# Attention and two feed-forward layers: three places each for keys, queries and values, loads asked for when free, scores first in a step, x's parts apart, later exponents in a buffer of their own

## The chip, the cores and the metric

The kernel runs on one core of a Trainium2 chip. The metric is the device time of one execution in microseconds (us). The core has five engines with instruction queues of their own, each worked off in program order: TensorE (PE, matrix products; its weight loads are shown as PEld), VectorE (DVE), ScalarE (ACT), GpSimd (POOL) and SyncE (SP), which here issues all DMA loads. An instruction that must wait for another engine holds everything behind it on its own engine. Matrix products land in PSUM, which has eight banks here called 0 to 7; everything else lies in SBUF.

## The reference

Windowed attention over 2 batches, 8 heads, 768 positions, head size 64, then two feed-forward layers. Cut to what matters:

```python
scores = scale * q @ k.T                  # per batch and head
keep = (key < n_global) | ((0 <= rel) & (rel < n_local))      # n_global 8, n_local 96
scores = where(keep, scores - slope[h] * dist, -1e9)
a = exp(scores - max(scores)); a = a / (sum(a) + 1e-9)
x = (a @ v) laid out as 1536 tokens x 512
h = x @ w_in;  x = (h * tanh(softplus(h))) @ w_out            # first layer, d_ff 2048
h = x @ w_in2; g = 0 if h <= -1, h if h >= 1, else (h + 1)**2 / 4
out = g @ w_out2                                              # second layer, d_ff 2048
```

The weights come as 64-bit floats, viewed as int64.

## The kernel before

**Attention.** Two heads make a pair; there are eight pairs (four per batch), and each takes three steps of two query blocks of 128, so the loop has 24 steps and runs from s = -1 to 27 (L383). The first block of a sequence sees 128 keys, all others 256 (`keys`, L302). A step passes through a pipeline whose stages work on different steps in one turn of the loop: in turn s, PE multiplies the transposed weights of step s-3 with the values (`values`, L376), transposes the weights of step s-2 (`transposes`, L358) and makes the scores of step s+1 (`scores`, L321), in this order. The scores have two pairs of PSUM banks, (0, 1) and (6, 7), used in turn. DVE adds the bias and takes the minimum (`softmax`, L333); ACT takes the exponential with its sum (L338); DVE makes the reciprocal of the sum of step s-1 (`normalise`, L343 and L344) and POOL multiplies with it (L348); ACT and DVE copy the transposed weights from PSUM, the first block by ACT, the second by DVE (`evict`, L363). A product of weights and values that is complete for 512 or 256 tokens is put on the list `done`; at the end of the same turn `split` (L407) rounds it to a high part on ACT (`rounded`, L169) and makes the low part, the remainder, on DVE (`remainder`, L174): x_hi and x_lo.

**Loads.** `load_qk` brings the keys and queries of a pair, `load_v` its values (L95, L96, L101). Pair (0, 0) has its keys and queries in a pool of its own; all else takes places in `a_raw`, two per kind (L283). Ahead of the loop stand the keys and queries of pair 1 and the values of pairs 0 and 1. In the loop, turn s = 3i asks for keys and queries of pair i+1 and turn 3i+2 for values of pair i+1; so the values of pair 1 are asked for a second time, in turn 2. SP issues the loads in program order, and a load waits until its place is free.

**Weights.** A weight tile holds 128 columns of w_in and 128 rows of w_out as 64-bit words; there are 16 for each layer. `Weights.load` (L201) brings one into one of two places (`stage`; a third place for tile 2), and `convert` makes float32 from the words in two halves i: `top` scales the upper 32 bits (L161, or on POOL L165), in place; `low` makes the bits that are shifted in from below (L223, ACT); `sign` takes the sign bit from the top 16 bits of the same word (L227, DVE); `value` combines the three in `wbits` (L230, DVE); `high` rounds (L169) and `rest` makes the remainder (L174). `wbits` has two places, taken in turn; the second also holds the distance tables of the attention bias at first. Three tiles (PRE) are converted inside the attention loop, at the turns that BESIDE (L36) lists: Tfi, Bfi, Vfi, Hfi and Rfi are top, low, sign with value, high and rest of half i of tile f; b2 to b7 are biases of heads, h and g the first pieces of the feed-forward part. On POOL are top and rest there (FIRST_ON); for tiles 3 to 15 top and high are on ACT and rest on DVE (LATER_ON).

**Feed-forward.** Each layer and batch takes 16 hidden tiles f; in period n PE makes h of tile n (L509, L510, L512, 768 tokens as 512 and 256) and the output products of tile n-1 (L560 in the first layer, L569 in the second). The gate of a tile of the first layer (`mish`) is a chain over ACT and DVE: exponential (L518), L520 and L521 on DVE, logarithm (L522) and exponential (L524) on ACT, the product with h on DVE (L525), and the product of the two (L528) on DVE; then ACT rounds g (L547) and DVE makes its remainder (L549). L525 is the last to read h, and frees its banks for the next tile. Tiles 3 to 15 of the first layer are converted beside the gates of the first 13 periods (`due`, L675), in three portions: after L525 come `begin` (the last tile's second rounding, top 0, low 0, sign 0), after L528 `middle` (the last tile's second remainder, value 0), after L549 `end` (top 1, low 1, sign 1, high 0, value 1, the next load, rest 0). Each engine runs these in the order in which the program writes them.

## Time and profile before

| what | us |
|---|---|
| three runs | 656.35, 651.24, 654.9 |
| their median | 654.9 |
| the profiled execution | 658.07 |
| its span, first to last instruction | 656.3 |
| busy in the span: PE, PEld, DVE, ACT, POOL | 622.4, 519.5, 414.7, 394.6, 57.7 |
| mean granted clock of TensorE, as a share of full speed | 0.988 |

The profile is of one execution. Busy time is the time in which an engine has an instruction in work; instructions overlap a little on one engine, so a group's sum can be more than the time that it takes. "Idle before" in a row is the time in which the engine had nothing to do just before that instruction, with the instruction that ended the wait behind an arrow. A wait for several things is put down to the one that came last.

### The profile page before, as it was taken

What the parts mean: (1) busy time and instruction counts of PE and PEld (TensorE: products, weight loads), DVE (VectorE), ACT (ScalarE), POOL (GpSimd) and SP (SyncE); (2) the same over time, 40 slices, a digit from 0 to 9 for tenths busy, and PEclk for the clock granted to TensorE, in tenths of its full rate; (3) what the DMA queues carried; (4) which work ended last, traced back from release to release, by engine and by line L of the source; (5) the groups of instructions that cost most, each with busy time, mean ns of one, the idle gap of its engine ahead of it and who ended that gap; (6) DMA issues with size and microseconds to landing.
All of it is one profiled execution on the core that took longest, in us unless ns stands there. A gap on an engine that the chain in (4) does not pass through costs nothing.

```text
span 656.3 us, 9854 instructions
## 1 busy us (share of the span) xinstructions
PE 622.4 (95%) x3600; PEld 519.5 (79%) x3600; DVE 414.7 (63%) x1019; ACT 394.6 (60%) x892; POOL 57.7 (9%) x122
## 2 busy tenths in 40 slices
PE   5687979999999999999999999999999999999996
PEld 4465657887877788888888888888888888888885
DVE  6487875888888897777777764766643433333332
ACT  5478874877787766666666665777733433333333
POOL 3546752000000000000000000000000000000000
PEclk9899989999999999999999999999999999999999
DMA  7955630133223310211111110233100100000002
GB/s 243 261 166 162 190 109 1 65 128 129 88 105 129 129 65 1 65 64 57 54 53 52 56 52 22 108 128 129 64 1 1 61 36 0 1 1 0 1 1 100
DMA packets 10567, 50.58 MB, mean 77 GB/s; under 512 B 1424, under 2 KB 1680, under 8 KB 6416
## 3 DMA queue, kind: packets, MB, share of 16 engines
q1 hardware_dynamic: 10512, 49.88, 23.1%
q8 instruction: 30, 0.49, 0.3%
q14 instruction: 25, 0.20, 0.1%
HBM read 46.73 MB, written 3.15 MB: 76 GB/s over the span
## 4 chain that ended last, share of the span: by engine, by line
PE 68%; DVE 16%; ACT 9%; DMA 3%; issue 2%; SPq 1%; POOL 0%; DVEq 0%; ACTq 0%; POOLq 0%
PE psum L569 20%; PE psum L560 12%; PE psum L509 11%; PE psum L510 11%; PE psum L512 10%; DVE wbits L230 3%; DVE e L521 3%; DVE wlo L174 2%; ACT pr L338 2%; DVE wbits L227 2%; DVE g_lo L549 2%; ACT qr L524 2%; PE psum L376 2%; PE psum L358 2%; DMA qr<-in_q_dram 2%
## 5 line engine op out<-in xcount | busy, mean ns | idle before, releaser
L534 DVE TENSOR_SCALAR e<-e 128x512 f32<-128x512 f32 x64 | 23.0, 360 | 121.3 <-ACT e L533 121.3
L533 ACT ACTIVATE e<-psum 128x512 f32<-128x512 f32 x64 | 30.8, 481 | 96.8 <-PE psum L512 96.8
L509 PE MATMUL psum<-x_hi,whi 128*128 128x512 f32 (+1 forms) x256 | 83.6, 343 | 3.7 <-DVE e L525 3.7
L509 PE MATMUL psum<-y_hi,whi 128*128 128x512 f32 (+1 forms) x256 | 82.4, 338 | 0.0
L510 PE MATMUL psum<-x_lo,whi 128*128 128x512 f32 (+1 forms) x256 | 82.3, 338 | 0.0
L510 PE MATMUL psum<-y_lo,whi 128*128 128x512 f32 (+1 forms) x256 | 82.0, 336 | 0.0
L569 PE MATMUL psum<-whi,g_hi 128*128 128x512 f32 x192 | 75.1, 391 | 0.0
L569 PE MATMUL psum<-wlo,g_hi 128*128 128x512 f32 x192 | 75.1, 391 | 0.0
L569 PE MATMUL psum<-whi,g_lo 128*128 128x512 f32 x192 | 74.7, 389 | 0.0
L549 DVE TENSOR_TENSOR g_lo<-e,g_hi 128x512 fp32r<-128x512 f32 (+1 forms) x128 | 65.5, 552 | 12.8 <-ACT g_hi L547 12.8
L547 ACT ACTIVATE g_hi<-e 128x512 fp32r<-128x512 f32 (+1 forms) x128 | 60.1, 517 | 22.3 <-DVE e L528 14.4
L560 PE MATMUL psum<-g_lo,whi 128*128 128x512 f32 (+1 forms) x256 | 69.2, 351 | 0.3
L560 PE MATMUL psum<-g_hi,whi 128*128 128x512 f32 (+1 forms) x256 | 65.8, 338 | 0.0
L560 PE MATMUL psum<-g_hi,wlo 128*128 128x512 f32 (+1 forms) x256 | 65.7, 338 | 0.0
L338 ACT ACTIVATE pr<-pr,st 128x256 f32<-128x256 f32 (+1 forms) x96 | 45.9, 480 | 26.5 <-DVE st L333 26.4
L509 PEld LDWEIGHTS psum<-x_hi,whi 128*128 128x128 f32 x256 | 48.3, 189 | 13.8 <-DVE e L525 7.4
L512 PE MATMUL psum<-x_hi,wlo 128*128 128x512 f32 (+1 forms) x256 | 54.9, 336 | 0.0
L512 PE MATMUL psum<-y_hi,wlo 128*128 128x512 f32 (+1 forms) x256 | 54.8, 336 | 0.0
L509 PEld LDWEIGHTS psum<-y_hi,whi 128*128 128x128 f32 x256 | 48.3, 189 | 7.8 <-DVE e L538 1.7
L510 PEld LDWEIGHTS psum<-y_lo,whi 128*128 128x128 f32 x256 | 48.5, 189 | 6.0
L510 PEld LDWEIGHTS psum<-x_lo,whi 128*128 128x128 f32 x256 | 48.5, 189 | 5.4
L518 ACT ACTIVATE e<-psum 128x512 f32<-128x512 f32 x64 | 29.7, 488 | 37.7 <-PE psum L512 37.1
(75 smaller groups left out, 1149.6 us busy)
## 6 DMA issues: line engine op xcount, KB each, us to landing
stage<-in_w_dram SPq DMA_DIRECT2D x31, 1024.0 KB, 4.9
vr<-in_v_dram SPq DMA_DIRECT2D x9, 704.0 KB, 5.2
out_dram<-stage SPq DMA_DIRECT2D x12, 256.0 KB, 2.7
kr<-in_k_dram SPq DMA_DIRECT2D x14, 216.0 KB, 5.9
qr<-in_q_dram SPq DMA_DIRECT2D x7, 384.0 KB, 6.4
third<-in_w_dram SPq DMA_DIRECT2D x1, 1024.0 KB, 8.3
kr<-in_k_dram SPq DMA_DIRECT2D x2, 144.0 KB, 2.8
qr<-in_q_dram SPq DMA_DIRECT2D x1, 256.0 KB, 2.9
```

The costliest lines, as they stand in the source:

```text
L230: nc.vector.scalar_tensor_tensor(out[:, i].bitcast(U32), words(U32, i, 1), 3, out[:, i].bitcast(U32), op0=ALU.logical_shift_left, op1=ALU. ...
L338: nc.scalar.activation(pr[:, u, j, 0:n], pr[:, u, j, 0:n], AF.Exp, scale=-1.0, bias=st[:, 0, u, j:j + 1], accum_out=st[:, 1, u, j:j + 1])
L509: nc.tensor.matmul(ph, wh[:, c], xh[:, c, tok], start=(c == 0), stop=False)
L510: nc.tensor.matmul(ph, wh[:, c], xl[:, c, tok], start=False, stop=False)
L512: nc.tensor.matmul(ph, wl[:, c], xh[:, c, tok], start=False, stop=(c == KD - 1))
L518: nc.scalar.activation(e, ph, AF.Exp)
L533: nc.scalar.activation(e, ph, AF.Relu, scale=0.5, bias=0.5)
L534: nc.vector.tensor_scalar(e, e, 1.0, None, op0=ALU.min)
L547: nc.scalar.activation(hi[:, t0:t0 + n], e, AF.Copy)
L549: nc.vector.tensor_tensor(lo[:, t0:t0 + n], e, hi[:, t0:t0 + n].bitcast(F32), op=ALU.subtract)
L560: nc.tensor.matmul(y, lhs[:, w], rhs[:, t0:t0 + n], start=(f == 0 and i == 0 and c % share == 0), stop=(f == NF - 1 and i == 2 and c % sha ...
L569: nc.tensor.matmul(ys[c], lhs[:, w], rhs, start=(f == 0 and i == 0), stop=(f == NF - 1 and i == 2))
```

## The change

- `a_raw` has three places for each kind. Ahead of the loop stand, in this order, keys and queries of pair 1, values of pair 0, keys and queries of pair 2, values of pairs 1 and 2. In the loop, turn 3i+2 asks for keys and queries of pair i+3, and turn 3i (from 6 on) for values of pair i+1; the second load of pair 1's values is gone. The first three weight tiles are asked for in turns 0, 4 and 10 (before 1, 6 and 10), the next two behind V11 and V21 (before R11 and R21).
- In a turn PE's order is scores, transposes, values.
- The rounding of x (x_hi) of what the last turn completed is ACT's first work in a turn; the remainder (x_lo) stands on DVE behind the first two scores and the reciprocal.
- `wbits` has one place. A new buffer `wsc` holds the bias tables at first; for tiles 3 to 15 `top` writes the scaled upper words there and `value` reads them there. For tiles 0 to 2 `top` stays in place.
- BESIDE is set anew; in `end` the next load stands ahead of `high(0)`.
- The eps tile goes: 1e-9 is added by a `tensor_scalar`, and the four numbers of a row of `st` lie side by side.

```diff
--- before.py
+++ after.py
@@ -34,10 +34,10 @@
 
 
 BESIDE = {
-    1: ("b2", "b3"), 3: ("b4",), 4: ("b5", "T00"), 5: ("T01",), 6: ("b6",), 7: ("b7", "B00"), 8: ("V00", "B01"),
-    9: ("V01", "H00"), 10: ("H01", "R00"), 11: ("R01",), 12: ("T10", "B10"), 13: ("T11", "V10", "B11"),
-    14: ("V11", "H10"), 15: ("R10", "H11"), 16: ("R11",), 17: ("T20", "B20"), 18: ("T21", "V20", "B21"),
-    19: ("V21", "H20"), 20: ("R20", "H21"), 21: ("R21",),
+    1: ("b2", "b3"), 3: ("b4",), 4: ("b5",), 5: ("T00",), 6: ("b6", "T01", "B00"), 7: ("b7", "V00", "B01"),
+    8: ("V01", "H00"), 9: ("H01", "R00"), 11: ("R01", "T10", "B10"), 12: ("T11", "V10", "B11"),
+    13: ("V11", "H10"), 14: ("R10", "H11"), 16: ("R11",), 17: ("T20", "B20"), 18: ("T21", "V20", "B21"),
+    19: ("V21", "H20"), 20: ("R20", "H21"), 22: ("R21",),
     24: ("h0a",), 25: ("h0b", "g0a"), 26: ("g0b", "h1a", "g0c"), 27: ("h1b",),
 }
 
@@ -111,11 +111,12 @@
     nc.scalar.preload_act_table_set("natural_log_exp_and_others")
     WU = 2 * DM
     stage = [wst.tile([P, WU], I64, name=f"stage{i}") for i in range(2)]
-    wbits = [wst.tile([P, 2, 2 * DM], U16, name=f"wbits{i}") for i in range(2)]
-
-
-
-    tables = wbits[1].rearrange("p a n -> p (a n)").bitcast(F32)
+    wbits = wst.tile([P, 2, 2 * DM], U16, name="wbits")
+    wsc = wst.tile([P, 2, DM], F32, name="wsc")
+
+
+
+    tables = wsc.rearrange("p a n -> p (a n)")
     dist, rel, col, away = (tables[:, a * P:b * P] for a, b in ((0, 3), (3, 5), (5, 6), (6, 7)))
     prev, shared, own, own0 = slice(0, PW), slice(PW, P), slice(P, 2 * P), slice(2 * P, 3 * P)
 
@@ -205,18 +206,23 @@
 
             hi, lo = (pool.tile([P, 2, DM], F32R, tag=f"w{n}{f}", name=f"w{n}{m}_{f}") for n in ("hi", "lo"))
             self.parts[m, f] = (hi, lo)
-            out = wbits[f % 2]
+            first = m == 0 and f < PRE
+            out = wbits
 
             def words(dtype, i, k):
                 n = 8 // mybir.dt.size(dtype)
                 return self.landing(m, f).bitcast(dtype).rearrange("p (a n w) -> p a n w", a=2, w=n)[:, i, :, k]
 
             bits = out.rearrange("p a (n two) -> p a n two", two=2)
-            on = FIRST_ON if m == 0 and f < PRE else LATER_ON
+            on = FIRST_ON if first else LATER_ON
+
+            def moved(i, dtype):
+
+                return words(dtype, i, 1) if first else wsc[:, i].bitcast(dtype)
 
             def top(i):
 
-                scaled(on[i], words(F32, i, 1), words(F32, i, 1), 2.0 ** -112)
+                scaled(on[i], moved(i, F32), words(F32, i, 1), 2.0 ** -112)
 
             def low(i):
 
@@ -227,7 +233,7 @@
                 nc.vector.tensor_scalar(bits[:, i, :, 1], words(U16, i, 3), 0x8000, None, op0=ALU.bitwise_and)
 
             def value(i):
-                nc.vector.scalar_tensor_tensor(out[:, i].bitcast(U32), words(U32, i, 1), 3,
+                nc.vector.scalar_tensor_tensor(out[:, i].bitcast(U32), moved(i, U32), 3,
                                                out[:, i].bitcast(U32),
                                                op0=ALU.logical_shift_left, op1=ALU.bitwise_or)
 
@@ -258,9 +264,9 @@
                 top(1)
                 low(1)
                 sign(1)
+                self.load()
                 high(0)
                 value(1)
-                self.load()
                 rest(0)
                 self.late = [lambda: high(1), lambda: rest(1)]
 
@@ -280,15 +286,15 @@
     def attention_windows(x_hi, x_lo, bank, wts, opening):
         with ExitStack() as es:
             cp = es.enter_context(tc.tile_pool(name="a_const", bufs=1))
-            rp = es.enter_context(tc.tile_pool(name="a_raw", bufs=2))
+            rp = es.enter_context(tc.tile_pool(name="a_raw", bufs=3))
             pp = es.enter_context(tc.tile_pool(name="a_p", bufs=2))
             sp = es.enter_context(tc.tile_pool(name="a_s", bufs=3))
-            load_qk(rp, 0, 1)
-            vs = {(0, 0): load_v(rp, 0, 0)}
-            vs[0, 1] = load_v(rp, 0, 1)
+            vs = {}
+            for p in range(3):
+                if p < 2:
+                    load_qk(rp, 0, p + 1)
+                vs[0, p] = load_v(rp, 0, p)
             bias = cp.tile([P, H, 3 * P], F32, name="bias")
-            eps = cp.tile([P, 2, 2], F32, name="eps")
-            nc.vector.memset(eps, 1e-9)
 
             def bias_of(h):
                 scaled(BIAS_ON[h], bias[:, h], dist, -slopes[h] / scale * FAR)
@@ -325,7 +331,7 @@
                 b, p, t = steps[s]
                 if u == 0:
                     probs[s] = (pp.tile([P, 2, 2, 2 * P], F32, tag="pr", name=f"pr{s}", bufs=3),
-                                sp.tile([P, 4, 2, 2], F32, tag="st", name=f"st{s}", bufs=3))
+                                sp.tile([P, 2, 2, 4], F32, tag="st", name=f"st{s}", bufs=3))
                 pr, st = probs[s]
                 n = keys(2 * t + u)
                 for j, ps in enumerate(scs[s]):
@@ -333,19 +339,19 @@
                     nc.vector.tensor_tensor_reduce(
                         pr[:, u, j, 0:n], ps[:, u, 0:n], bias[:, h, 0:n] if n > P else bias[:, h, 2 * P:],
                         scale=-scale, scalar=3e38, op0=ALU.add, op1=ALU.min,
-                        accum_out=st[:, 0, u, j:j + 1],
+                        accum_out=st[:, u, j, 0:1],
                     )
                     nc.scalar.activation(pr[:, u, j, 0:n], pr[:, u, j, 0:n], AF.Exp, scale=-1.0,
-                                         bias=st[:, 0, u, j:j + 1], accum_out=st[:, 1, u, j:j + 1])
+                                         bias=st[:, u, j, 0:1], accum_out=st[:, u, j, 1:2])
 
             def normalise(s):
                 pr, st = probs[s]
-                nc.vector.tensor_tensor(st[:, 2], st[:, 1], eps, op=ALU.add)
-                nc.vector.reciprocal(st[:, 3], st[:, 2])
+                nc.vector.tensor_scalar(st[..., 2], st[..., 1], 1e-9, None, op0=ALU.add)
+                nc.vector.reciprocal(st[..., 3], st[..., 2])
                 for u in range(2):
                     n = keys(2 * steps[s][2] + u)
                     for j in range(2):
-                        nc.gpsimd.tensor_scalar(pr[:, u, j, 0:n], pr[:, u, j, 0:n], st[:, 3, u, j:j + 1], 1.0,
+                        nc.gpsimd.tensor_scalar(pr[:, u, j, 0:n], pr[:, u, j, 0:n], st[:, u, j, 3:4], 1.0,
                                                 op0=ALU.mult, op1=ALU.mult)
 
             def transposes(s):
@@ -381,34 +387,37 @@
             for h in range(2):
                 bias_of(h)
             for s in range(-1, NU + 4):
-                if s in (1, 6, 10):
+
+                if s in (0, 4, 10):
                     wts.load()
-                if s > 0 and s % 3 == 0 and s // 3 + 1 < len(pairs):
-                    load_qk(rp, *pairs[s // 3 + 1])
-                if s > 0 and s % 3 == 2 and s // 3 + 1 < len(pairs):
+                if s >= 2 and s % 3 == 2 and s // 3 + 3 < len(pairs):
+                    load_qk(rp, *pairs[s // 3 + 3])
+                if s >= 6 and s % 3 == 0 and s // 3 + 1 < len(pairs):
                     vs[pairs[s // 3 + 1]] = load_v(rp, *pairs[s // 3 + 1])
+                ready, done[:] = done[:], []
+                for hi, lo, src in ready:
+                    rounded("a", hi, src)
+                if s + 1 < NU:
+                    scores(s + 1)
+                if 0 <= s - 2 < NU:
+                    transposes(s - 2)
                 if 0 <= s - 3 < NU:
                     values(s - 3)
-                if 0 <= s - 2 < NU:
-                    transposes(s - 2)
-                if s + 1 < NU:
-                    scores(s + 1)
                 if 0 <= s < NU:
                     softmax(s, 0)
                 if 0 <= s - 1 < NU:
                     normalise(s - 1)
+                for hi, lo, src in ready:
+                    remainder("v", lo, src, hi)
                 if 0 <= s - 2 < NU:
                     evict(s - 2, 0)
                 if 0 <= s < NU:
                     softmax(s, 1)
                 if 0 <= s - 2 < NU:
                     evict(s - 2, 1)
-                for hi, lo, src in done:
-                    split(hi, lo, src)
-                done[:] = []
                 for name in BESIDE.get(s, ()):
                     opening[name]()
-                    if name in ("R11", "R21"):
+                    if name in ("V11", "V21"):
                         wts.load()
 
 
...
```

## Rows read from the trace of the kernel before

**Rows 1.** The page's busy times: us (share of the span) xinstructions of each engine.
```profile
PE 622.4 (95%) x3600; PEld 519.5 (79%) x3600; DVE 414.7 (63%) x1019; ACT 394.6 (60%) x892; POOL 57.7 (9%) x122
```

**Rows 2.** Windows: stretch, length, busy us (xinstructions) by engine, PEclk, DMA share, GB/s.
```profile
250.15:258.57 8.42, 8.42 (x50) 7.37 (x49) 7.88 (x17) 6.78 (x16) 0.00 (x0) 1.00 0.00 0
129.83:241.73 111.90, 107.90 (x578) 88.13 (x577) 93.95 (x192) 82.44 (x165) 0.00 (x0) 1.00 0.33 113
```

**Rows 3.** Windows of the attention loop: groups of three steps, and one slow stretch.
```profile
14.14:29.46 15.32, 9.49 (x91) 7.01 (x91) 7.50 (x33) 8.50 (x31) 7.88 (x17) 0.91 0.98 300
...
40.87:52.98 12.11, 9.12 (x90) 6.56 (x90) 9.88 (x40) 9.70 (x33) 6.71 (x14) 1.00 0.70 226
...
88.03:98.91 10.88, 9.55 (x83) 7.14 (x83) 8.12 (x36) 8.67 (x31) 7.72 (x15) 0.84 0.18 72
sum 84.77, PE 67.77 PEld 49.61 DVE 61.30 ACT 62.59 POOL 49.77; mean PE 9.68 PEld 7.09 DVE 8.76 ACT 8.94 POOL 7.11
...
27.87:32.84 4.97, 4.97 (x29) 3.66 (x29) 1.43 (x10) 1.57 (x6) 2.12 (x5) 0.50 0.84 186
```

**Rows 4.** Waits from 28 to 99 us: us in total, times, longest.
```profile
ACT pr L338 <- DVE st L333: 19.0, 15, 5.4
...
PE psum L376 <- ACT pts L169: 10.8, 9, 2.3
DVE x_lo L174 <- ACT x_hi L169: 10.7, 11, 1.4
```

**Rows 5.** Timeline about one split: start, us, engine, line, operation, operands [idle before].
```profile
49.90 0.58 ACT L169 ACTIVATE x_hi<-psum 128x512 fp32r<-128x512 f32 x1
...
50.51 0.69 DVE L174 TENSOR_TENSOR x_lo<-psum,x_hi 128x512 fp32r<-128x512 f32 x1 [1.21 <-ACT x_hi L169]
...
51.11 0.41 DVE L333 CUSTOM_DVE_ANT_0 pr<-psum,bias 128x256 f32<-128x256 f32 x1
...
51.57 0.51 ACT L338 ACTIVATE pr<-pr,st 128x256 f32<-128x256 f32 x1 [0.58 <-DVE st L333]
```

**Rows 6.** The chain that ended last: start, us, what.
```profile
17.29 10.54 DMA qr<-in_q_dram
```

**Rows 7.** Timeline of PE: the scores behind that load.
```profile
27.87 1.66 PE L321 MATMUL psum<-kr,qr 64*128 64x128 f32 x8 [5.83 <-DMA qr<-in_q_dram]
```

**Rows 8.** The page's DMA issues: xcount, KB each, median us to landing.
```profile
stage<-in_w_dram SPq DMA_DIRECT2D x31, 1024.0 KB, 4.9
vr<-in_v_dram SPq DMA_DIRECT2D x9, 704.0 KB, 5.2
...
kr<-in_k_dram SPq DMA_DIRECT2D x14, 216.0 KB, 5.9
qr<-in_q_dram SPq DMA_DIRECT2D x7, 384.0 KB, 6.4
```

**Rows 9.** Timeline of SP: the values asked for a second time.
```profile
15.76 0.33 SPq L101 DMA_DIRECT2D vr<-in_v_dram  x1
```

**Rows 10.** Timeline of ACT and DVE in one feed-forward period.
```profile
210.17 0.65 ACT L161 ACTIVATE stage<-stage 128x512 f32<-128x512 f32 x1
...
210.85 0.47 DVE L227 TENSOR_SCALAR wbits<-stage 128x512 uint16<-128x512 uint16 x1 [1.34 <-ACT stage L161]
211.21 1.02 DVE L528 TENSOR_TENSOR e<-e,qr 128x512 f32<-128x512 f32 x2
211.93 0.94 ACT L547 ACTIVATE g_hi<-e 128x512 fp32r<-128x512 f32 x2 [0.42 <-DVE e L528]
```

**Rows 11.** Timeline of POOL: the second scaling of weight tile 0 (T01).
```profile
24.55 0.65 POOL L165 TENSOR_SCALAR stage<-stage 128x512 f32<-128x512 f32 x1
```

**Rows 12.** All additions of eps: duration ns min/median/max, first and last start us.
```profile
L343 DVE TENSOR_TENSOR st<-st,eps x24: 148/156/1297, 10.0 to 100.5; 128x4 f32<-128x4 f32 x24
```

**Rows 13.** Timeline of POOL and DVE at the longest addition.
```profile
69.86 1.28 POOL L174 TENSOR_TENSOR wlo<-wbits,whi 128x512 fp32r<-128x512 f32 x1
69.86 1.30 DVE L343 TENSOR_TENSOR st<-st,eps 128x4 f32<-128x4 f32 x1
```

## Prediction: what the change will do

> **What bounds the kernel now.** I read the page first: TensorE (PE) is busy for 622.4 of 656.3 us [rows 1], so time can come only from stretches in which PE waits. Windows over the span show two. From about 250 us on, PE runs unbroken in a fixed rhythm; nothing that the change touches lies on that path. The two stretches are the attention loop (to 99 us) and the first batch in the first feed-forward layer, where twelve hidden tiles take 111.90 us [rows 2].
>
> *The attention loop.* Every third step's value products (twelve matmuls of L376) mark groups of three steps, one for each pair of heads. The seven groups from 14.14 to 98.91 us take 84.77 us; PE is busy 67.8, ScalarE (ACT) 62.6 and VectorE (DVE) 61.3 us in them [rows 3]. No engine fills the stretch. The waits say for what they stand: DVE's remainder of x waits for ACT's rounding of x 10.7 us in 11 pieces, ACT's exponentials wait for DVE's scores-plus-bias 19.0 us, PE's value products wait for ACT's copy of the transposed weights 10.8 us [rows 4]. Rounding and remainder stand at the end of a step: DVE idles 1.21 us until ACT has rounded, subtracts, and only then starts the next step's scores, for which ACT in its turn idles 0.58 us [rows 5]. Two engines, each some 75% full, take turns.
>
> *The load.* The queries of pair 2 are asked for at 17.29 us and land 10.54 us later [rows 6]. PE starts their scores at 27.87 us after 5.83 us of idling [rows 7], and then runs at a granted clock of 0.50, the 1.2 GHz level, until 32.84 us [rows 3]. What is ahead of them is long: values of 704 KB are loaded nine times for eight pairs and weight tiles hold 1024 KB [rows 8]; the ninth load is pair 1's, asked for again at 15.76 us [rows 9].
>
> *The feed-forward stretch.* Twelve periods take 111.90 us, 9.3 us each, while the period from 250.15 us, with the same matmuls, takes 8.42 us at an unbroken PE [rows 2]. The timeline shows why: DVE's sign extraction (L227) waits 1.34 us for ACT's exponent scaling (L161), because L161 writes the word in place and L227 reads two of those bytes. DVE's product (L528) is queued behind it, and ACT's rounding of g (L547) then waits 0.42 us for that product [rows 10].
>
> **The change, part by part.** The sum is made against the profiled execution: 658.07 us, the span and 1.8 us around it, 3.2 us above the median of 654.9.
>
> *Loads.* Pair 2's keys and queries now stand in front of pair 1's values, with no repeated values and no weight tile ahead. Before, from 5.8 us on, 4.9 MB lay in the queue up to and including pair 2's queries: pair 1's keys and queries 0.84, values 0.72 three times, a weight tile 1.05, pair 2 0.84 [rows 8]. Landed at 27.83 us, that is 222 GB/s. Now 2.4 MB lie there: about 16.6 us. PE is ready for step 6's scores at 22.04 us now (27.87 less 5.83) and, as they move ahead of two of a step's three blocks, near 20 us then; so the stall goes, and with it the slow clock, in which 4.97 us hold half as much work (2.5 us). The price moves to the first weight tile: at 222 GB/s it lands near 27.8 us, at the 300 GB/s of the first group [rows 3] near 23 us, while POOL's first scaling now stands where the second stood, at 24.55 us [rows 11]. So POOL may stand up to 3.3 us, the next normalisation queued behind it, for which PE's transposes wait. The lower end is nothing; I take 1 us, between the two, as the transposes have a step's lead. The later loads have six steps of lead: nothing.
>
> *x's parts apart.* The rounding becomes ACT's first work in the next step, while DVE adds the bias; the remainder follows DVE's first two scores and the reciprocal, by when ACT has rounded. The wait of 10.7 us goes, and what ACT loses behind it. Two scores are now queued behind the remainder, for which ACT has two exponentials in hand.
>
> *Scores first.* S(s+1), T(s-2), V(s-3) replaces V, T, S (scores, transposes, values). No matmul is added. The value products stand two blocks later, some 2 us, and PE's 10.8 us of waiting for their copies came in nine pieces of 1.2 us on average [rows 4]. In front of T and V now stands the wait of S(s+1) for DVE's last scores of step s-1; in the list of waits no such wait stands out, and the cost is counted as nothing (above: rival 4).
>
> *Conversions earlier, one wbits.* No instruction more or less in the loop, so its totals stay. The sign-and-value pairs fall into steps 7-8, 12-13 and 18-19.
>
> *Small operands.* The memset of eps goes; tensor_scalar replaces tensor_tensor on 128x4. That addition takes 156 ns in the median and 1297 at most [rows 12], the longest beside a POOL subtraction of 1.28 us [rows 13]. The new form is not in the trace; bounded by those two, I take the median and count nothing. The Trainium skill (SBUF — State Buffer, Who interferes with whom) says that a DVE instruction with two SBUF inputs is held by a POOL instruction that reads SBUF, and so is tensor_scalar in a two-port mode. The long row agrees with the first; by the second this edit gains nothing, by the first alone the 1.14 us of that row.
>
> *The loop's sum.* A group with one tile's signs and values keeps DVE busy 9.9 us; PE needs 9.1 us at full clock, and without a conversion DVE and ACT stay below that (8.12, 8.67) [rows 3]. Three groups of 9.9 and four of 9.1 make 66.1 us: the floor. Handoffs stay: 0.03 us from ACT's rounding to the remainder, 0.05 us from a score to its exponential [rows 5]; three such in a step's round, 0.15 us, are 3.2 us in 21 steps. With 1 us for POOL: 70.3 us. Gain 84.8 - 70.3 = 14.5 us; bounds 18.7 (the floor) and about 8 (only the stall, 5.8, and its slow clock, 2.5).
>
> *wsc.* For tiles 3 to 15 the sign no longer reads what the scaling writes. DVE runs on at 209.51 instead of 210.85 us, the product ends over 1 us earlier, and ACT's wait of 0.42 us goes. DVE's work is 7.8 us per period (93.95 in twelve), under PE's 8.42 [rows 2], so PE sets the period: 111.90 - 12 x 8.42 = 10.9 us. The scaling into another buffer is not in the trace: nearest is the one in place, 0.65 us [rows 10]; at twice that, two of them add 1.3 us to ACT's 6.9 us per period, still under 8.42, and below it nothing is gained, so I take 0.65. One wbits makes the next tile's low words wait for the last remainder, which DVE ends a third of a period before: nothing. The lower bound: if only ACT's 0.42 us go, 12 x 0.42 = 5 us.
>
> Sum: 14.5 + 10.9 = 25.4 us. 658.07 - 25.4 = 632.7 us for an execution like the profiled one; 654.9 - 25.4, so 630 us, for a median.
>
> **Rivals.**
> 1. *DVE becomes the bound of the feed-forward period.* 7.8 us of work leave 0.6 us for its waits on ACT. Then 5 us are gained there: 635 us. For it: DVE still needs ACT's low words and exponentials. Against: ACT has 82.4 of 111.9 us of work [rows 2].
> 2. *The loop keeps taking turns*, and only the stall goes (8 us): 636 us. For it: in conversion steps ACT waits for DVE's own work. Against: the x pieces are the link in [rows 5].
> 3. *The loads bind still*: POOL's first scaling or step 6's scores wait the whole 3.3 us: 632 us.
> 4. *Slower: scores first.* If DVE's last scores of step s-1 come late, PE stands in front of S(s+1) while T and V could run, and DVE then waits for T. It decides from 1.2 us in each of 21 steps, which eat the 25.4 us; at 1.6 us the time is 663 us. For it: DVE is the fullest engine in conversion groups. Against: between one step's last score and the next use of T's result DVE has a copy and two more scores of 0.41 us [rows 5].
> 5. *It doesn't do what it says*: a hazard on the single wbits takes the sign's place, and POOL's wait holds the loop: 650 us.
>
> **Numbers.** Forecast 0.68; rivals 0.10, 0.12, 0.04, 0.03, 0.03. About 1% is what a measurement here can tell from no change. The forecast and rivals 1 to 3 are faster by more (0.94, of which I leave 0.01 to the same): faster 0.93, same 0.04, slower 0.03. The range: floor and full period (18.7 + 10.9), with 3 us more for the 1.8 us around the span and port waits, give 622; the low gains on both (8 + 5) give 642.
>
> **What would show it.** Right: no DMA wait of PE after 10 us and step 6's scores near 21 us; no wait of the remainder on the rounding of x; groups of 9 to 10.5 us; the last group's value products near 84 us; the sign waiting for nothing in the feed-forward stretch, and periods of 8.42 us from the second tile on. Wrong: a POOL wait near 25 us; PE waiting in front of L321; a period near 9 us; a DVE wait on wbits.

## The result, and the profile after

| what | us |
|---|---|
| before, median of four runs | 654.88 (651.24 to 656.35) |
| after, median of four runs | 630.54 (629.22 to 631.40) |
| ratio | 0.9635, 95% interval 0.9592 to 0.9677 |
| profiled execution before / after | 658.07 / 630.53 |
| its span before / after | 656.3 / 628.6 |

The forecast was 630. The medians differ by 24.3 us; the profiled pair by 27.5, because before's profiled execution was 3.2 us above its median. Through the whole result it has to be kept apart which of the two a number belongs to.

The page of after, busy time by engine and two of its rows of 40 slices:

```profile
PE 612.2 (97%) x3600; PEld 519.5 (83%) x3600; DVE 420.4 (67%) x1018; ACT 392.3 (62%) x892; POOL 59.0 (9%) x122
...
PE   5999999999999999999999999999999999999996
...
PEclk9999999999999999999999999999999999999999
```

PE is busy at 90% or more in every slice between the first and the last (97% of the span, where [rows 1] had 95%), and its granted clock has no dip. A line through two instants of the program splits the saved 27.7 us of span. The first output product of the first layer started at 112.62 us before and starts at 97.36 us after: 15.3 us come from the attention loop and its tail. From there to the output products of the last tile of the first layer's first batch (241.73 us before, 215.50 after) it was 129.1 us and is 118.1: 11.0 us. The remaining 1.5 us lie behind that; nothing in the prediction speaks of them, and no run followed them up.

**The loop.** Windows of after: seven groups of three steps from value products to value products, their sum, and twelve periods of the feed-forward stretch (length; busy us and instructions of PE, PEld, DVE, ACT, POOL; granted clock; DMA share; GB/s):

```profile
16.24:24.93 8.69, 8.69 (x92) 6.59 (x91) 8.05 (x37) 7.93 (x30) 5.85 (x14) 1.00 1.02 340
24.93:35.84 10.91, 10.07 (x91) 6.57 (x90) 9.14 (x36) 9.24 (x30) 8.04 (x15) 1.00 1.03 286
35.84:45.09 9.25, 9.25 (x92) 7.18 (x91) 9.15 (x36) 9.20 (x34) 7.95 (x15) 1.00 1.02 303
45.09:56.00 10.91, 9.88 (x92) 7.46 (x91) 10.67 (x40) 9.86 (x33) 8.41 (x15) 1.00 0.73 223
56.00:65.40 9.40, 9.40 (x92) 7.20 (x91) 9.20 (x38) 8.52 (x31) 7.50 (x15) 1.00 0.60 192
65.40:76.20 10.80, 9.55 (x92) 7.17 (x91) 10.56 (x40) 9.78 (x33) 7.25 (x14) 1.00 0.33 138
76.20:84.73 8.53, 7.57 (x75) 5.64 (x75) 8.20 (x33) 7.68 (x28) 6.54 (x13) 1.00 0.00 1
16.24:84.73 68.49, 64.41 (x615) 47.82 (x615) 64.95 (x252) 62.21 (x212) 51.53 (x99) 1.00 0.68 213
105.94:206.98 101.04, 101.04 (x579) 88.42 (x578) 95.55 (x195) 85.30 (x168) 0.00 (x0) 1.00 0.37 127
```

Against [rows 3], 84.77 us became 68.49, and DVE, 72% full before, is busy for 64.95 of them, 95%. These groups gave 16.3 us, but the first of them starts 2.1 us later than before (16.24 against 14.14 us). In two of the three longest groups DVE works 10.67 of 10.91 and 10.56 of 10.80 us: it is the bound there. The last row is 12 x 8.42 us.

Waits of after in the loop's seven groups (total, times, longest):

```profile
ACT pr L344 <- DVE st L339: 3.8, 8, 0.9
...
POOL stage L166 <- DMA stage<-in_w_dram: 3.0, 1, 3.0
...
PE psum L327 <- DVE st L339: 2.2, 3, 1.0
```

The long entries of [rows 4] are gone or small: ACT's exponentials wait 3.8 us for DVE's scores where it was 19.0, and the remainder of x no longer appears. New are POOL's wait for a weight tile and PE's for DVE in front of the scores, 2.2 us of idling PE.

Timeline of after, around one early turn (start, duration, engine and line, what it does; a bracket would show idling before it):

```profile
20.15 0.93 PE L327 MATMUL psum<-kr,qr 64*128 64x128 f32 x8
...
20.34 0.58 ACT L170 ACTIVATE x_hi<-psum 128x512 fp32r<-128x512 f32 x1
...
20.95 0.69 DVE L175 TENSOR_TENSOR x_lo<-psum,x_hi 128x512 fp32r<-128x512 f32 x1
...
25.96 0.67 POOL L166 TENSOR_SCALAR stage<-stage 128x512 f32<-128x512 f32 x1 [3.05 <-DMA stage<-in_w_dram]
```

Step 6's scores start at 20.15 us and wait for no load ([rows 7] had them at 27.87 after 5.83 us of idling). ACT rounds x while DVE is still at scores; the remainder follows 0.03 us after the rounding, without a bracket, where [rows 5] had 1.21. And POOL's first scaling of a weight tile waits 3.05 us.

**The feed-forward stretch.** Timeline of after, one period:

```profile
175.62 0.46 DVE L233 TENSOR_SCALAR wbits<-stage 128x512 uint16<-128x512 uint16 x1
...
175.97 1.01 DVE L537 TENSOR_TENSOR e<-e,qr 128x512 f32<-128x512 f32 x2
...
176.48 0.65 ACT L162 ACTIVATE wsc<-stage 128x512 f32<-128x512 f32 x1
...
177.68 0.91 ACT L556 ACTIVATE g_hi<-e 128x512 fp32r<-128x512 f32 x2
```

The sign (L233) now starts before the scaling (L162) of its half has even begun; the product (L537) follows at once, and ACT's rounding of g waits for nothing. [rows 10] had 1.34 and 0.42 us there. The scaling into its own buffer takes 0.65 us, as the one in place did.

### The profile page after: what moved, and what is told of

The parts are those of the page before. It is cut to its first block, busy times and chain, and to the rows that moved or that the text cites. A ratio compares the mean times of both kernels' runs of the same rounds, so it can differ in the third digit from the quotient of the medians.

```text
span 628.6 us, 9915 instructions
## 1 busy us (share of the span) xinstructions
PE 612.2 (97%) x3600; PEld 519.5 (83%) x3600; DVE 420.4 (67%) x1018; ACT 392.3 (62%) x892; POOL 59.0 (9%) x122
## 4 chain that ended last, share of the span: by engine, by line
PE 87%; DVE 8%; issue 1%; ACT 1%; POOL 1%; SPq 1%; DMA 0%; DVEq 0%; POOLq 0%; ACTq 0%
PE psum L569 22%; PE psum L578 21%; PE psum L518 14%; PE psum L519 14%; PE psum L521 14%; DVE pr L339 3%; DVE pts L172 1%; PE psum L364 1%; DVE st L349 1%; PE psum L327 1%; DVE wbits L236 1%; DVE x_lo L175 1%; ACT pr L344 1%; POOL pr L354 1%; PE psum L382 1%
## 5 line engine op out<-in xcount | busy, mean ns | idle before, releaser
L542 ACT ACTIVATE e<-psum 128x512 f32<-128x512 f32 x64 | 30.8, 481 | 103.8 <-PE psum L521 103.8
L518 PE MATMUL psum<-x_hi,whi 128*128 128x512 f32 (+1 forms) x256 | 82.3, 338 | 0.0
L527 ACT ACTIVATE e<-psum 128x512 f32<-128x512 f32 x64 | 31.3, 490 | 57.9 <-PE psum L521 57.4
L569 PE MATMUL psum<-g_lo,whi 128*128 128x512 f32 (+1 forms) x256 | 67.4, 344 | 0.0
L556 ACT ACTIVATE g_hi<-e 128x512 fp32r<-128x512 f32 (+1 forms) x128 | 59.3, 511 | 10.5 <-DVE e L537 6.3
```

The lines of the kernel that those rows point to most:

```text
L518: nc.tensor.matmul(ph, wh[:, c], xh[:, c, tok], start=(c == 0), stop=False)
L527: nc.scalar.activation(e, ph, AF.Exp)
L542: nc.scalar.activation(e, ph, AF.Relu, scale=0.5, bias=0.5)
L556: nc.scalar.activation(hi[:, t0:t0 + n], e, AF.Copy)
L569: nc.tensor.matmul(y, lhs[:, w], rhs[:, t0:t0 + n], start=(f == 0 and i == 0 and c % share == 0), stop=(f == NF - 1 and i == 2 and c % sha ...
```

## The experiments

The parts of the change touch different stretches, so they can be taken apart. The theory: the saved time is 10.9 us from wsc and 14.5 us from the loop, the latter from the loads and from x's parts. The rivals were that one of these does nothing, that scores first costs time, and that the additions and the first weight tile's wait hold back part of the gain. The additions are those of 1e-9 to the sums of the exponentials. All medians below are of four to six runs. Runs of before beside them gave medians of 653.0 to 653.7 us.

**wsc alone.** The kernel before with the buffer wsc and one wbits, nothing else:

```diff
-    wbits = [wst.tile([P, 2, 2 * DM], U16, name=f"wbits{i}") for i in range(2)]
+    wbits = wst.tile([P, 2, 2 * DM], U16, name="wbits")
+    wsc = wst.tile([P, 2, DM], F32, name="wsc")
...
-                scaled(on[i], words(F32, i, 1), words(F32, i, 1), 2.0 ** -112)
+                scaled(on[i], moved(i, F32), words(F32, i, 1), 2.0 ** -112)
```

> The kernel before, with wsc and the single wbits alone; loop, loads and order as before. Theory (the sign no longer waits for the scaling, PE sets the period): twelve periods of 8.42 us, 11 to 12.5 us less than before, about 643 us. Rival 1 of the prediction (DVE's own work or a hazard on the one wbits binds): periods of about 9 us, 5 us less, about 650 us. The attention loop should keep its 84.8 us.

Measured: 642.27 us against 653.5, ratio 0.9822 (0.9795 to 0.985): 11.2 us. Its trace has twelve periods in 101.04 us, 8.42 us each, as after has. This part is settled, mechanism and size: the step's 10.9. The run shows something else besides. Its loads and the order of its turn are before's, yet PE waits for step 6's queries for only 2.21 us (its rows stand further down), and its first output product starts at 107.89 us, 4.7 earlier than in before's profile, without any edit to loads or order. So the stall of 5.83 us in [rows 7] was larger than the same loads gave in this other execution, which fits before's profile standing 3.2 us above its median. The 25 runs of before beside the experiments point the same way: at a mean granted clock of 0.999 they took 650.89 to 651.59 us (four runs), at 0.991 653.22 to 657.26 (eight), at 0.986 659.17. So what the stall and its slow clock cost seems to differ from execution to execution, by some 8 us between the fastest and the slowest.

**x's parts at the end of the turn again.** After, with rounding and remainder back together:

```diff
-                ready, done[:] = done[:], []
-                for hi, lo, src in ready:
-                    rounded("a", hi, src)
...
-                for hi, lo, src in ready:
-                    remainder("v", lo, src, hi)
...
+                for hi, lo, src in done:
+                    split(hi, lo, src)
+                done[:] = []
```

> The changed kernel with rounding and remainder of x back at the end of the turn. Theory (the x pieces make ACT and DVE take turns): the remainder waits for the rounding again, about 0.5 to 1 us in each of 14 turns; 5 us or more over the changed kernel, 636 to 640 us. Rival (scores first carries the loop, the x pieces are hidden): within 1 us of the changed kernel, 631 us.

Measured: 639.39 us, ratio 0.9768 (0.9742 to 0.9794), 8.9 us above after. The waits of this kernel over its loop (its profiled execution took 642.23 us, the longest of its five):

```profile
DVE x_lo L175 <- ACT x_hi L170: 14.5, 14, 1.9
...
ACT pr L344 <- DVE st L339: 13.8, 14, 1.8
...
PE psum L327 <- DVE st L339: 7.7, 7, 2.3
```

The chain of the prediction is back link by link, and with scores first PE hangs on it too. One turn of it in the timeline:

```profile
56.98 0.69 DVE L175 TENSOR_TENSOR x_lo<-psum,x_hi 128x512 fp32r<-128x512 f32 x1 [1.03 <-ACT x_hi L170]
...
59.20 0.51 ACT L344 ACTIVATE pr<-pr,st 128x256 f32<-128x256 f32 x1 [1.74 <-DVE st L339]
...
60.12 0.48 PE L327 MATMUL psum<-kr,qr 64*128 64x256 f32 x1 [1.98 <-DVE st L339]
```

DVE idles 1.03 us, ACT 1.74 after it, PE 1.98 after that.

**Scores last.** After, with PE's blocks in the old order:

```diff
-                if s + 1 < NU:
-                    scores(s + 1)
-                if 0 <= s - 2 < NU:
-                    transposes(s - 2)
                 if 0 <= s - 3 < NU:
                     values(s - 3)
+                if 0 <= s - 2 < NU:
+                    transposes(s - 2)
+                if s + 1 < NU:
+                    scores(s + 1)
```

> The changed kernel with PE's old order: values, transposes, scores. Theory (with the x pieces apart the copies come in time, so the order is worth little): 0 to 3 us over the changed kernel, 631 to 634 us. Rival (the order carries the loop: the value products wait for ACT's copies again): 5 to 10 us over it, 636 to 640 us. If scores first costs time (rival 4 of the prediction), it is faster than the changed kernel.

Measured: 632.79 us, ratio 0.9667 (0.964 to 0.9693), 2.3 us above after by the medians; its first output product starts at 99.70 us, also 2.3 later. A small gain of scores first: the four runs (631.72 to 633.20 us) all lie above after's four, though the intervals of the ratios overlap. Rival 4 (it costs) is out.

**The old loads.** After, with two places and the old order and turns of the loads:

```diff
-            rp = es.enter_context(tc.tile_pool(name="a_raw", bufs=3))
+            rp = es.enter_context(tc.tile_pool(name="a_raw", bufs=2))
...
-                if s in (0, 4, 10):
+                if s in (1, 6, 10):
                     wts.load()
-                if s >= 2 and s % 3 == 2 and s // 3 + 3 < len(pairs):
-                    load_qk(rp, *pairs[s // 3 + 3])
-                if s >= 6 and s % 3 == 0 and s // 3 + 1 < len(pairs):
+                if s > 0 and s % 3 == 0 and s // 3 + 1 < len(pairs):
+                    load_qk(rp, *pairs[s // 3 + 1])
+                if s > 0 and s % 3 == 2 and s // 3 + 1 < len(pairs):
                     vs[pairs[s // 3 + 1]] = load_v(rp, *pairs[s // 3 + 1])
```

> The changed kernel with two places per kind and the loads in the old order and turns, the repeated values of pair 1 among them. Theory (the stall of step 6 and its slow clock are worth 8 us): scores of step 6 start near 28 us again, 637 to 639 us. Rival (the loop makes up for a late start, since DVE binds later): 631 to 633 us.

Measured: 647.35 us, ratio 0.9893 (0.9862 to 0.9924), 16.8 us above after, well over what was expected. Waits of PE and of SP's queue in this kernel's loop:

```profile
PE psum L325 <- DMA qr<-in_q_dram: 13.2, 4, 4.7
...
SPq L101 <- PE psum L380: 55.5, 6, 13.1
```

Three lines of its timeline:

```profile
29.70 0.33 SPq L101 DMA_DIRECT2D vr<-in_v_dram  x1
...
31.70 0.58 SPq L96 DMA_DIRECT2D qr<-in_q_dram  x1
...
40.33 1.74 PE L325 MATMUL psum<-kr,qr 64*128 64x128 f32 x8 [4.70 <-DMA qr<-in_q_dram]
```

PE waits four times, not once. With scores first the queries are wanted earlier; with values last a place for values comes free later. SP works its list in order: it stands in front of a load of values until PE's value products have freed a place (55.5 us in six waits), the queries are asked for behind it, 2 us after the values are, and their scores start 8.6 us after that, 4.70 of which PE idles. Such waits of SP are in before too (50.5 us in six); what changes is when they end. The same load of values is asked for at 21.15 us in the kernel with wsc alone and at 29.70 here, just after the value products of step 2, which now stand behind step 6's late scores; from 24 to 30 us the DMA engines are busy for only 1%. The old loads and the new turn make a loop of their own: late values hold the queue, late queries hold PE.

**The new loads with the old turn.** This left the question of what the loads are worth by themselves. After, with both edits of the turn (scores first, x apart) undone, that is the two diffs above together:

> The changed kernel with both edits of the turn's order undone: values, transposes, scores, and the split of x at the turn's end; loads, conversions and wsc as changed. Against the kernel with wsc alone (642.3 us) it shows what loads and conversions bring in the old turn, against the one with scores last (632.8 us) what the x pieces bring. Theory (the stall with its slow clock is worth 8 us in the old turn, so the old loads cost 16.8 us in the new turn because scores first sharpens the need): 633 to 636 us, the x pieces 1 to 3 us. Rival (the loads are worth some 16 us in either turn): 626 to 628 us. Second rival (the x pieces are worth some 9 us without scores first too): 640 to 642 us, and the loads almost nothing.

Measured: 643.05 us, ratio 0.9855 (0.9819 to 0.9892). All four have wsc; wsc alone has besides the old turns of the weights' conversions and the old addition, which go with the old loads there, while the old loads in the new turn have after's:

| median us | old turn | new turn |
|---|---|---|
| old loads | 642.27 | 647.35 |
| new loads | 643.05 | 630.54 |

In the old turn the new loads, with the conversions' turns and the addition, bring nothing (0.8 us, inside the intervals; a gain of one part that another eats is not excluded); in the new one they are worth 16.8. And the new turn with old loads is 5 us worse than the old turn. Why nothing, when the stall of step 6's scores goes? Timelines of PE around it, first in wsc alone (old loads, old turn):

```profile
14.01 0.88 PE L380 MATMUL psum<-pts,vr 128*64 128x128 f32 x12 [0.20 <-DMA vr<-in_v_dram]
...
24.13 0.93 PE L325 MATMUL psum<-kr,qr 64*128 64x128 f32 x8 [2.21 <-DMA qr<-in_q_dram]
24.98 1.12 PE L380 MATMUL psum<-pts,vr 128*64 128x128 f32 x12
```

then with the new loads and the old turn, and a window of the same kernel (columns as above):

```profile
15.95 1.12 PE L382 MATMUL psum<-pts,vr 128*64 128x128 f32 x12 [1.80 <-DMA vr<-in_v_dram]
...
25.36 0.93 PE L327 MATMUL psum<-kr,qr 64*128 64x128 f32 x8
...
26.77 1.17 PE L382 MATMUL psum<-pts,vr 128*64 128x128 f32 x12 [0.48 <-ACT pts L170]
```

```profile
15.95:18.00 2.05, 2.05 (x17) 1.72 (x18) 0.10 (x2) 0.00 (x0) 1.93 (x5) 0.62 0.98 362
```

The stall didn't go, it moved. In both kernels the values of pair 0 are asked for at 7.6 us; where pair 2's keys and queries and more values are asked for right behind them, they land 8.2 us later instead of 6.3, the first value products wait 1.80 us and start at 15.95 instead of 14.01 us, and after this idling the slow clock (0.62 granted on average, so in part the 1.2 GHz level) follows there instead of behind step 6. Step 3's value products, the start of the next group, come 1.8 us later than with the old loads. From them on both loops take about the same for six groups (69.2 and 68.5 us): they still take turns, as the waits of the kernel with new loads and old turn say:

```profile
ACT pr L344 <- DVE st L339: 15.8, 15, 1.8
DVE x_lo L175 <- ACT x_hi L170: 13.3, 13, 1.7
```

Each kernel is read here from one execution, but the landing is the same in all traces: from asking to landing pair 0's values take 6.0 to 6.4 us in the three with the old loads (before, wsc alone, old loads) and 7.2 to 8.2 us in the eight with the new ones. The kernel with scores last starts its first value products at 15.50 us, followed by the slow clock too; before starts them at 14.14 [rows 3]. In after the first value products stand behind scores and transposes, start at 16.24 us and wait for no load; that is where the new turn hides what the new loads make late.

**The addition.** After's additions stand out in the list of their line (min/median/max in ns):

```profile
L349 DVE TENSOR_SCALAR st<-st x24: 158/170/1108, 10.2 to 84.2; 128x4 f32<-128x4 f32 x24
```

In the timeline:

```profile
54.59 1.28 POOL L175 TENSOR_TENSOR wlo<-wbits,whi 128x512 fp32r<-128x512 f32 x1
...
54.80 1.10 DVE L349 TENSOR_SCALAR st<-st 128x4 f32<-128x4 f32 x1
```

Six of the 24 take 1.03 to 1.11 us instead of 0.17, one beside each of POOL's six remainders of weights, and each ends just behind it (55.90 against 55.87 us here). All 24 take 10.5 us; before it was 5.8, with four that ended so: the one of 1.30 us in [rows 13], and three of 0.40 to 0.46 us that began late in a remainder. Two kernels ask whether the form is to blame, or the addition. In one the reciprocal reads the sum itself (the sum holds exp(0) = 1, so 1e-9 changes no bit of it); in the other tensor_tensor with the tile eps is back:

```diff
-                nc.vector.tensor_scalar(st[..., 2], st[..., 1], 1e-9, None, op0=ALU.add)
-                nc.vector.reciprocal(st[..., 3], st[..., 2])
+                nc.vector.reciprocal(st[..., 3], st[..., 1])
```

> The changed kernel without the addition of 1e-9: the reciprocal reads the sum itself (the sum holds exp(0) = 1, so in float32 the addition changes no bit). In the changed kernel's trace six of the 24 additions take 1.03 to 1.11 us, each beside a POOL subtraction, where the usual one takes 0.17. Theory (DVE sets the loop's end, and the addition is held by POOL): six times 0.9 us and up to 18 times 0.17 us come off DVE, 4 to 7 us less than the changed kernel, 623.5 to 626.5 us. Rival (the holds sit in slack, or the next instruction of DVE is held in the addition's place): 629 to 631 us.

```diff
-                nc.vector.tensor_scalar(st[..., 2], st[..., 1], 1e-9, None, op0=ALU.add)
+                nc.vector.tensor_tensor(st[..., 2], st[..., 1], eps, op=ALU.add)
```

> The changed kernel with the eps tile and the tensor_tensor form of the addition. Theory (a POOL subtraction holds either form, and it is the new order that puts the additions beside the subtractions): within 1 us of the changed kernel, 630.5 us, with five or six additions of over 1 us. Rival (the scalar form is held and the old one is not): 3 to 5 us less, 626 to 627 us.

Measured: 626.47 us without the addition (0.9571, 0.954 to 0.9601), 4.1 below after; 630.96 with tensor_tensor (0.9634, 0.9602 to 0.9665), the same as after. The list of the line in the kernel with tensor_tensor:

```profile
L351 DVE TENSOR_TENSOR st<-st,eps x24: 153/164/1106, 10.1 to 83.8; 128x4 f32<-128x4 f32 x24
```

The kernel without the addition, its reciprocal's line, one stretch of its timeline, and three windows:

```profile
L349 DVE RECIPROCAL st<-st x24: 169/176/181, 10.1 to 80.1; 128x4 f32<-128x4 f32 x24
```

```profile
37.41 1.28 POOL L175 TENSOR_TENSOR wlo<-wbits,whi 128x512 fp32r<-128x512 f32 x1
...
37.64 0.18 DVE L349 RECIPROCAL st<-st 128x4 f32<-128x4 f32 x1
```

```profile
24.74:35.61 10.87, 10.08 (x91) 6.58 (x91) 8.88 (x33) 9.28 (x31) 8.01 (x15) 1.00 1.02 292
...
54.62:63.31 8.69, 8.69 (x91) 6.59 (x90) 7.45 (x35) 8.69 (x33) 8.09 (x17) 1.00 0.66 201
63.31:73.15 9.84, 9.10 (x91) 6.90 (x91) 9.17 (x35) 9.15 (x31) 6.43 (x13) 1.00 0.39 161
```

Both forms of addition are held to the end of POOL's subtraction; the reciprocal in the same place is not. The five groups of after in which an addition is held get shorter, the two here from 9.40 to 8.69 and from 10.80 to 9.84 us; the two without stay (8.69, and 10.91 against 10.87). So the held ones seem to be what costs; all 24 additions were taken out at once, and the shares were not measured apart.

Why six for over 1 us now and one before? The kernel with x's parts at the end of the turn has the same additions and the same turns for the conversions. Its timeline:

```profile
49.40 1.29 POOL L175 TENSOR_TENSOR wlo<-wbits,whi 128x512 fp32r<-128x512 f32 x1
49.46 0.42 DVE L175 TENSOR_TENSOR x_lo<-psum,x_hi 128x256 fp32r<-128x256 f32 x1 [0.77 <-ACT x_hi L170]
...
50.22 0.49 DVE L349 TENSOR_SCALAR st<-st 128x4 f32<-128x4 f32 x1
```

No addition there is over 0.49 us, and all take 5.4. DVE is at the remainder of x when POOL's subtraction begins; with x apart DVE reaches the addition 0.2 us after that beginning and stands almost the whole of it. So x apart pays this price out of its own gain. The order of PE has a part in it: with scores last four additions, not six, take over 1 us.

**The first weight tile earlier**, ahead of pair 1's values, so that POOL doesn't wait:

```diff
+                if p == 1:
+                    wts.load()
                 vs[0, p] = load_v(rp, 0, p)
...
-                if s in (0, 4, 10):
+                if s in (4, 10):
```

> The changed kernel with the first weight tile asked for ahead of the values of pair 1. Theory (POOL's wait of 3.0 us for the tile delays the normalisation and PE's transposes of the next turns): POOL's wait goes, the group of steps 6 to 8 falls from 10.9 to about 10 us, 1 us less, 629.5 us. Rival (the wait is hidden, or the values of pair 1 come late instead): no change or up to 1 us more.

Measured: 630.13 us (0.9632, 0.9598 to 0.9666), by the median 0.4 below after, which is inside the intervals. In its profiled execution (629.17 us) POOL's first scaling starts at 22.58 us without a wait, the group in which it stood falls from 10.91 to 9.59 us, and the first output product starts 1.35 us earlier. So of the wait of 3.05 us more than half was hidden, as a step's lead suggested; what the rest is worth in the median stays open, as the six runs spread from 628.87 to 633.13 us.

**Both**, without the addition and with the first tile earlier:

> No addition and the first weight tile earlier, together. Theory: the two gains add, 5 to 8 us less than the changed kernel, 622.5 to 625.5 us. Rival: what e5 gives alone.

Measured: 624.86 us, ratio 0.9553 (0.9522 to 0.9585): 5.7 us below the changed kernel, the fastest of the study, and 1.6 below the one without the addition, where the intervals overlap.

## Why the prediction was right, point by point

*The time.* 630 was forecast for the median and 632.7 for an execution like the profiled one; 630.5 came for both. Of the signs named for it, these are in the lists above: no DMA wait of PE after 10 us, step 6's scores at 20.15 us (near 21), no wait of the remainder, the last value products at 84.73 (near 84), the sign waiting for nothing, periods of 8.42 us from the second tile on. The groups are from 8.5 to 10.9 us where 9 to 10.5 was named. Three signs listed as "wrong" are there too, all small: POOL's wait near 25 us, PE's in front of the scores, 2.2 us in three pieces, and a DVE wait on wbits, for ACT's low words: 2.3 us in nine pieces over 13 periods, none over 0.3, and PE's period doesn't show it. The sum was right, its shares were not, and part of its nearness is luck. 630 is the median less a gain read from an execution 3.2 us above that median; the profiled pair itself gained 2.1 us more than its forecast, 27.5 against 25.4. And 84.73 us is near 84 because two errors cancel: the first group starts 2.1 us later than the forecast took it, and the seven take 1.8 us less.

*wsc: right in mechanism and size.* 10.9 us forecast, 11.0 in the profiled pair, 11.2 alone. Rival 1 (DVE bounds the period) is out: DVE is busy 95.55 of 101.04 us, and PE's period is unbroken. So is rival 5 (a hazard on the single wbits).

*Loads: the step that was mis-sized.* It put the stall (5.8 us) and its slow clock (2.5) down as a gain. In the old turn the edit brings nothing: 643.05 against 642.27 us. Three things failed in it. One execution's stall was taken for the usual one; another with the same loads had 2.2 us, and the runs of before at a granted clock of 0.999 take some 651 us. It let the bytes that lay ahead set the landing: 4.9 MB from 5.8 to 27.83 us, 222 GB/s. A window of before over this time:

```profile
5.80:27.83 22.03, 14.64 (x120) 10.26 (x117) 14.37 (x69) 14.69 (x55) 11.42 (x25) 0.98 0.94 304
```

At 304 GB/s the DMA engines moved 6.7 MB; at most 0.6 of the 1.8 MB more can have been left of earlier loads (144 KB twice and 256 KB), so by this estimate over 1 MB went to loads asked for behind the queries. And the queries were asked for only at 17.29 us because SP had stood 6.7 us in front of pair 1's second load of values until the first had landed. Last, it followed only the load that got earlier. It asked what lies ahead of pair 2's queries, 2.4 MB, and what became late behind them (the first weight tile), but not that with more loads behind them pair 0's values land later: 1.9 us in this pair of traces, at a place where PE needs them at once. It had the price at POOL; in the old turn it was at PE's first value products, with a slow clock of its own. Rival 2 (the loop keeps taking turns and only the stall goes, 8 us, 636) rests on the same term and is out, as ACT's waits for DVE fell from 19.0 to 3.8 us; rival 3 (the loads bind still) had the place wrong, and in after, with the values last, nothing of it is left but POOL's wait.

*x's parts apart: right, and the carrier of the loop.* Putting them back costs 8.9 us in after; doing it in the old PE order gains 10.3 us (643.05 to 632.79). The wait it removes was read as 10.7 us in [rows 4].

*Scores first: counted as costing nothing.* It gains 2.3 us beside x apart; with x together 3.7 by the medians and nothing by the profiles, so that size stays open. The parts don't add: undoing one each costs 8.9, 2.3 and 16.8 us, 28 in all, where the loop gained some 13 by the medians (24.3 less 11.2). The prediction priced the loads against the old turn's demand. Their worth is that the new turn asks for queries earlier and frees values later, so that it can't do without them. Whether the third place or the earlier asking does it was not separated.

*Additions: the step that was wrong.* It bounded the new form by 0.156 and 1.297 us and took the median; it compared forms and not places. The Trainium skill (SBUF — State Buffer, Who interferes with whom) says that a DVE operation with two SBUF inputs contends with a POOL operation that reads SBUF, that tensor_scalar in a two-port mode does too, the one that issues second waiting for the first, and that one with a single SBUF input outside these modes doesn't contend. The runs agree: 1.106 us for the longest tensor_tensor, 1.108 for tensor_scalar, 0.181 for the reciprocal; in which mode the tensor_scalar ran no run shows. The edit's change of form gained nothing, as the prediction said by that rule. What the step did not ask is which instruction of DVE would stand beside POOL's subtraction once the turn was reordered. It is this one, for up to 4.1 us, and two of the conversion groups came out at 10.9 and 10.8 us instead of 9.9 (without the addition 10.1 and 9.8).

*POOL's wait for the first tile.* 1 us was taken between 0 and 3.3; the wait is 3.05 us, and its price 0.4 (medians) to 1.35 (profiles). The lower of its two landings was worked out wrongly: 4.9 MB from 5.8 us at 300 GB/s end at 22.1 us, not 23. POOL went on at 25.96 us, between the two.

*How the loop's sum came out.* 70.3 us forecast, 68.5 measured. The single gains were off, the loads too high by up to 8 us in the old turn, the additions' price too low by up to 4; but the 70.3 did not rest on them. It was worked out as each group's fullest engine plus handoffs, and that held: in six of the seven groups of after one engine is busy for all but 0.33 us at most (PE 8.69 of 8.69, DVE 10.67 of 10.91, DVE 8.20 of 8.53). In it PE's floor was too high (9.1 us; it takes 8.69 for the same matmuls when nothing interrupts it) and DVE's in conversion groups too low (9.9 against 10.6 and 10.7, by the held additions), and the two errors largely cancelled.

## What to carry to other kernels

Where two engines take turns, estimate the end by the fullest engine of each stage rather than by adding up waits; the waits overlap, and one execution can show a stall over twice another's. Subtract a gain from the execution from which it was read. A load that is moved forward can delay those already under way, so ask of each of them where it is needed next; and judge order and loads together, since one fixes when places come free and the other when they are wanted. When work is reordered, look at which small instructions come to stand beside a long one of another engine that can hold them.

## What the runs showed of the hardware

A DVE operation on 128x4 elements can cost more than one on 128x512: tensor_scalar and tensor_tensor that began 0.2 to 0.3 us into POOL's subtraction of 1.28 us ran 1.03 to 1.11 us, six of 24 times, each to the end of the subtraction, against 0.69 for a remainder of 128x512; a reciprocal in the same place stayed at 0.18 us.

A load under way is slowed by loads asked for after it on the same queue. The values of pair 0, asked for at 7.6 us in every kernel, landed 6.0 to 6.4 us later with one more load of values and a weight tile behind them (three traces), and 7.2 to 8.2 us later where keys, queries and more values followed (eight traces). The DMA engines were busy for 0.99 of the time from 7.59 to 15.95 us in the kernel with wsc alone and in the one with new loads and old turn, but moved 357 GB/s in the first and 278 in the second; how much of the delay is the sharing and how much the lower rate was not separated.

A merged row can hide a wait. SP's two loads of pair 3's keys in after, the second of them by itself, and a line of SP's waits:

```profile
12.74 3.36 SPq L95 DMA_DIRECT2D kr<-in_k_dram  x2
...
15.64 0.47 SPq L95 DMA_DIRECT2D kr<-in_k_dram  x1
...
SPq L95 <- DMA vr<-in_v_dram: 3.4, 2, 2.2
```

Asking does not take 3.36 us: the first of the two takes 0.66 and the second starts at 15.64 us, just after pair 0's values have landed, for which SP waits. Eight loads were under way until then, and in none of the eleven traces are there ever more than eight; in after 13 loads are asked for with seven others still under way, in before two. What sets the eight, the chip or the program's own semaphores, is not shown. So in after "asked for when free" holds for the places, but not always for the queue.
